# Layer 2's four x sums formed apart, a superblock ahead, and kept in DRAM

## The chip, the cores and the metric

The kernel runs on one core of one Trainium2 chip. The metric is device time in microseconds (us) of one execution. Before the change the median of three runs is 1597.66 us (1596.65 to 1598.69).

## The reference

A linear attention is followed by two MLPs. Softmaxes of q (over its head dimension) and k (over the sequence) give, per batch and head, `kv = k_s.T @ v` and `out = q_s @ kv`; the result is x, 4608 tokens by 512. Then

```python
h = x @ moe_w_in              # 512 x 2048
x = max(0.01 * h, h) @ moe_w_out
h = x @ moe2_w_in
out = (h / (1 + exp(-h))) @ moe2_w_out
```

All inputs and the output are float32. The kernel calls the four products layers 0, 1, 2 and 3.

## The kernel before

**Arithmetic.** An operand of a product is held as a high part (a rounded copy, ScalarE) and a low part (what is left, a VectorE subtraction), so a float32 product is three matmuls on TensorE: high by high, high by low, low by high. Layers 1, 2 and 3 are done as 2 x 2 blocks by a scheme with seven products in place of eight. Each of the seven products c takes one block, or one sum of blocks, of the weights and one of x. For layer 2's x, products 1, 2 and 3 take blocks as they are, and products 7, 5, 6 and 4 take sums: 7 = 3 - 5', 5 = 5' - 1, 6 = 3 - 5, 4 = 2 - 6, where 5' is the raw fourth block (`SUMS["x"]`, line 720; 11 and 12 are second copies of raw blocks 1 and 2).

**Tiling.** Tokens come in nine blocks of 512, and layers 1 and 2 take them in superblocks n = 0 to 4: four of two blocks, and a last one of one block. A full superblock has for layer 2 two operands per product (kq = 0, 1, written 6a and 6b below), the last has one. In layer 2 (`layer2`, lines 1007 to 1044) a superblock has four turns i; a turn has seven products, in the order 1, 2, 6, 5, 7, 4, 3, where product 1 of the next turn is put ahead of products 4 and 3 of this one. A product is 12 matmuls.

**x of layer 2.** Layer 1's result goes to DRAM (`store1`, line 994, into `x2d`). `x_all` (line 816) takes, for each superblock, an operand tile for each product and kq from the pool `r_x`, in the order 1, 5, 3, 2, 6, 7, 4; `operand` (line 776) spawns the loads (`fetch`, line 737), the sums (`sums`, line 746, into 128 x 512 work tiles of the pool `r_o`) and the split (`split2`, line 757): a ScalarE copy to the high half (`copy`, line 302), a VectorE subtraction to the low half (`sub`, line 298). Sums are VectorE operations of `add` (line 863). Raw blocks wait in the low halves of tiles (`HOME2`, line 730: the copies 11 and 12 go to tiles 5 and 4). There are six loads per kq.

`r_x` has 15 tiles once layer 1 runs out: eight called x, three g, and xs, xv and two xr. Layer 2 holds 14 of them (seven per kq) for all four turns of a superblock, and gives each pair back after its product in the last turn (line 1042). `r_o` has 16 tiles.

**What sets the order.** The program of every engine is written out in an order that a planner finds (`Queues`, lines 63 to 146). Each piece of work is a generator with a rank; it yields operations with an engine and a cost ("D" is the DMA queue at 0.73 us per 256 KB, plus 3.0 us to landing), waits for named events, and takes tiles. At each step the operation that can begin first is taken, and among equals the one of lowest rank (line 122). `yield rank(r)` sets the rank and holds nothing back (line 100). Engines then run in that order, and a semaphore holds an instruction until what it needs is there. All loads and stores are issued by SyncE (the SP queue), in order.

Other work of the same stretches: `convert3` (line 431) turns the last layer's weights into blocks, in layer 1's gaps, and its two `raw` tiles join `r_x` as xr when it ends (line 435); `weight` (line 798) loads and splits a weight when its room comes free; `blocks1`, `blocks2`, `plus` and `active` take products out of PSUM; `keep` (line 1095) stores layer 2's result to `gd`.

Of the kernel before, what the change touches and what calls it, by code (L numbers as in the profile page):

```python
# [9 lines left out]
F32 = mybir.dt.float32  # L10
# [4 lines left out]
ALU = mybir.AluOpType  # L15
# [31 lines left out]
def rank(r):  # L47
    return "rank", r


def op(*engines):
    return "op", engines


def wait(*keys):
    return "wait", keys


def get(ring):
    return "get", ring  # L60


class Queues:
# [14 lines left out]
    def spawn(self, rank, gen):  # L78
        self.tasks.append([rank, next(self.count), self.now, gen, None, 0.0, None])
        self.tasks.sort(key=lambda t: t[:2])  # L80
        self.step(next(t for t in self.tasks if t[3] is gen), None)
# [8 lines left out]
    def done(self, key):  # L90
        self.events[key] = self.now
# [111 lines left out]
def linear_attention_two_mlps(  # L203
# [24 lines left out]
    nc = tc.nc  # L228
    B, H, S, D = q.shape
    NT, DM = out.shape  # L230
    DFF = w_in1.shape[1]
    P = 128
    TB = 512
    NB = NT // TB
    NP = H // 2
    KD = DM // P
# [25 lines left out]
    NJ = len(supers)  # L262
    width = [len(s) * HB for s in supers]
    merge = [2 // len(s) for s in supers]
    gd1 = [tc.dram_tile([NG, 2, 4, P, len(s), HB], F32, name=f"gda{n}") for n, s in enumerate(supers)]
    gd = [tc.dram_tile([NG, 4, len(s), P, 2, HB], F32, name=f"gd{n}") for n, s in enumerate(supers)]
    x2d = [tc.dram_tile([KD, P, 2, w], F32, name=f"x2d{n}") for n, w in enumerate(width)]

    NKV = 8
    NV = 2 * (D + 1)  # L270
# [11 lines left out]
    done, spawn = qs.done, qs.spawn  # L282
# [410 lines left out]
    def act(j, f, h):  # L693
# [28 lines left out]
    }  # L722
    ORDER = (1, 2, 6, 7, 5, 3, 4)
# [3 lines left out]
    SECOND = (2, 5, 3)  # L727
    HOME = {3: (6, 1), 5: (7, 1), 2: (4, 1)}
    HOMES = HOME, {}
    HOME2 = {11: (5, 0), 12: (4, 1)}  # L730
    slot = {}

    def raw_of(key, c, home):
# [42 lines left out]
    def operand(keys, kind, r, order, srcs, give, home={}, used=(), each=0.0):  # L776

        def turn(c):
            return r + each * used.index(c) if c in used else r

        for key in keys:
            spawn(r, sums(key, kind, home, turn))
        for c in order:
            for key, src in zip(keys, srcs):
                yield rank(r)
                slot[key, c] = yield from give(c)
                done(("slot", key, c))
                for d in src:
                    if home.get(d, (d, 1))[0] == c:
                        spawn(r, fetch(key, d, home, src[d]))  # L790
                spawn(turn(c), split2(key, kind, c, home))
# [6 lines left out]
    def weight(l, i, c):  # L798
# [14 lines left out]
        src = wc[l][2 * i:2 * i + 2, :, PLANS[l][2].index(c)].rearrange("r p n -> p r n")  # L813
        yield from operand([key], "", weight_rank(l, i, c), (c,), [{c: src}], give)

    def x_all():
        for n in range(NJ):

            r, pm = at2[n, 0] - (5 if n else 4), merge[n]
            yield rank(r)  # L820
            yield wait(*(("x2", n, k, t) for k in range(0, KD, pm) for t in range(2)))
            keys, srcs = [], []
            for kq in range(2 // pm):
                keys.append(("x", 2, n, kq))
                srcs.append({})
                for c, k, t in ((1, 0, 0), (5, 0, 1), (2, 1, 0), (3, 1, 1)):
                    at = 2 * k + kq * pm
                    srcs[-1][c] = x2d[n][at:at + pm, :, t].rearrange("k p w -> p k w")
                    if c < 3:
                        srcs[-1][10 + c] = srcs[-1][c]  # L830
            yield from operand(keys, "x", r, (1, 5, 3, 2, 6, 7, 4), srcs, lend, home=HOME2, used=ORDER, each=0.5)

    def g1_all():
        for n in range(NJ):
            pm = merge[n]
            for g, (cs, kind) in enumerate(((FIRST, "b"), (SECOND, ""))):
                for i in range(NG):
                    for q_ in range(2 // pm):
                        at = at1[n, g, i, q_] - 4
                        yield rank(at)  # L840
                        fs = range(4 * i + 2 * q_, 4 * i + 2 * q_ + 2 * pm)
                        yield wait(*(("gd1", j, f) for j in supers[n] for f in fs))
                        src = {
                            c: gd1[n][i, q_ * pm:(q_ + 1) * pm, m].rearrange("z p j n -> p z (j n)")
                            for m, c in enumerate(KEPT1)
                        }
                        yield from operand(
                            [("x", 1, n, g, i, q_)], kind, at, cs, [src], lend, home=HOMES[g]
                        )
# [11 lines left out]
    def add(o, a, b, alu=ALU.add):  # L861
        yield op(("V", v_tt(TB)))
        nc.vector.tensor_tensor(out=o, in0=a, in1=b, op=alu)  # L863
# [81 lines left out]
                                    spawn(-100, blocks1(n, mb))  # L945

    def blocks1(n, m):
        key, pm = (1, n), merge[n]

        def product(c):  # L950
            yield wait(("p", 1, n, m, c))
            return banks[key, m, c]

        def room():
            return (yield get(r_o))

        def end(c):
            r_b.put(banks.pop((key, m, c)))

        p = yield from product(1)  # L960
        s = yield from room()
        yield op(("A", a_(TB)))
        copy("A", s, p)
        done(("kept", n, m))
        p = yield from product(6)
        yield from add(s, s, p)
        end(6)
        p = yield from product(7)
        u = yield from room()
        yield from add(u, s, p)  # L970
        end(7)
        p = yield from product(4)
        t = yield from room()
        yield from add(t, u, p)
        end(4)
        spawn(-100, store1(n, 2 + m * pm, 0, t))
        p = yield from product(2)
        t = yield from room()
        yield op(("A", a_(TB)))
        copy("A", t, p)  # L980
        banks.pop((key, m, 1))
        end(2)
        spawn(-100, store1(n, m * pm, 0, t))
        p = yield from product(5)
        yield from add(u, u, p)
        spawn(-100, store1(n, 2 + m * pm, 1, u))
        yield from add(s, s, p)
        end(5)
        p = yield from product(3)
        yield from add(s, s, p)  # L990
        end(3)
        spawn(-100, store1(n, m * pm, 1, s))

    def store1(n, k, t, o):
        pm = merge[n]
        yield op(("D", 0.73))
        nc.sync.dma_start(
            out=x2d[n][k:k + pm, :, t].rearrange("k p w -> p k w"), in_=o.rearrange("p (k w) -> p k w", k=pm)
        )
        yield wait()  # L1000
        r_o.put(o)
        done(("x2", n, k, t))

    INTO = {1: 1, 6: 1, 7: 1, 4: 1, 2: 2, 5: 5, 3: 5}
    AFTER = {6: 1, 7: 6, 4: 7, 3: 5}
# [170 lines left out]
    for j in range(NB):  # L1176
        for i in range(NG):
            at3[j, i] = t_
            t_ += 2

    def weight_rank(l, i, c):
        if l == 1:
            return at1[0, int(c in SECOND), i, 0] - 8
        return (at2[0, i] if l == 2 else at3[0, i]) - 8

    with tc.manual_schedule():
        nc.vector.memset(ones, 1.0)
        make_identity(nc, ident)
        nc.scalar.activation(out=small[0]["k"][:, 0:1], in_=ones, func=ACTF.Exp)
        for t_, t in sets:  # L1190
            t5 = t.rearrange("p (c h d) -> p c h d", c=5, h=2)
            nc.gpsimd.memset(t5[:, :, :, D:], 1.0)

            nc.gpsimd.memset(t_[SR:P, 512:640], 0.0)
            nc.gpsimd.memset(t5[SR:P, 4, :, 0:D], 0.0)
        nc.gpsimd.memset(kv_tile, 0.0)

        for n in range(NP):
            r = -40 + 5 * n
            spawn(r, k_task(n))  # L1200
            spawn(r + 1, q_task(n))
            spawn(r + 2, v_task(n))
        for n in range(NP, len(units)):
            b, j, p = units[n]
            r = -12 + 3 * p if j == 1 else step(j, 0) - 14 + 4 * p
            if b is not None:
                spawn(r, k_task(n))
                spawn(r, v_task(n))
            spawn(r, q_task(n))
        for f in range(NF):  # L1210
            spawn(-36 + 6 * f if f < 4 else step(0, f) - 4, split1(f))
            if f < NH:
                spawn(f, layer0(0, f))
        spawn(0, layer0_all())
        for t in (convert1, convert2, convert3):
            spawn(1000, t())
        spawn(0, later())
        for i, c in lead:
            spawn(weight_rank(1, i, c), weight(1, i, c))
        for l in (2, 3):  # L1220
            for i in range(NG):
                for c in ORDER:
                    spawn(weight_rank(l, i, c), weight(l, i, c))
        spawn(base[1] - 4, g1_all())
        spawn(base[2] - 5, x_all())
        spawn(base[3] - 4, g3_all())
        spawn(base[1], layers())
        qs.run()
# [30 lines left out]
```

## Time and profile before

| | |
|---|---|
| median of three runs | 1597.66 us |
| the profiled execution, its own time | 1598.44 us |
| its span in the trace | 1596.7 us |
| mean granted TensorE clock, share of full | 0.995 |
| layer 2's first matmul starts | 855.14 us |
| layer 3's first matmul starts | 1229.78 us |

Times in the rows are from the start of the span. In the timelines a row is "start, length, engine, line, operation, output <- input, tiles' shape, count", and a bracket is the time for which the engine had been idle and what ended it. PE is TensorE, DVE VectorE, ACT ScalarE, SPq the queue of SyncE that issues DMAs. A clock of 0.50 is the lower of TensorE's two levels, 1.2 GHz; 1.00 is 2.4 GHz.

### The profile page before, as it was taken

To read this page: it belongs to the slowest core of one execution; us is meant where nothing else is said; L and a number is where in the kernel's file an instruction comes from. 1 tells how busy PE (TensorE), PEld (TensorE's weight loads), DVE (VectorE), ACT (ScalarE), POOL (GpSimd) and SP (SyncE) were. 2 spreads that over 40 slices of the span, in tenths; PEclk is the share of its full clock that TensorE was granted. 3 is DMA by queue.
4 is the path that set the end of the run, shared out by engine and by line. 5 is a ranking of instruction groups with operands and counts; after the bars stand their busy time and mean duration, and the time that the engine had idled before them with its cause. 6 is when DMAs were issued, how large, how long until landed. Compare 5 with 4: busy or idle time off the path is not lost.

```text
span 1596.7 us, 26548 instructions
## 1 busy us (share of the span) xinstructions
PE 1548.6 (97%) x9088; PEld 1340.4 (84%) x9088; DVE 1093.9 (69%) x2046; ACT 893.5 (56%) x1965; POOL 39.4 (2%) x56
## 2 busy tenths in 40 slices
PE   5899999999999999999997999999999999999999
PEld 3687888888788888888887878787889999999998
DVE  8986756665656988888888352525267777777774
ACT  7778776685445544454556454545467444444442
POOL 2111000000000000000000000000000000000000
PEclk9999999999999999999999999999999999999999
DMA  8876778786789787878797353535369444444442
GB/s 236 267 200 179 227 228 255 227 269 194 240 268 312 234 293 217 273 219 268 230 323 269 106 185 106 185 106 175 108 195 303 133 131 133 132 133 127 134 128 70
DMA packets 281190, 320.01 MB, mean 200 GB/s; under 512 B 61408, under 2 KB 208352, under 8 KB 281056
## 3 DMA queue, kind: packets, MB, share of 16 engines
q1 hardware_dynamic: 281056, 318.32, 63.8%
q8 instruction: 72, 1.18, 0.3%
q14 instruction: 62, 0.51, 0.1%
HBM read 201.85 MB, written 116.39 MB: 199 GB/s over the span
## 4 chain that ended last, share of the span: by engine, by line
PE 90%; DVE 6%; DMA 2%; SPq 1%; issue 1%; ACT 0%; POOL 0%; DVEq 0%; POOLq 0%; ACTq 0%
PE b L1124 12%; PE h L1124 11%; PE h L1034 10%; PE b L931 10%; PE h L931 10%; PE b L1034 8%; PE h L665 8%; PE h L667 8%; PE h L666 8%; DVE o L863 2%; PE a L637 2%; DVE x L298 1%; PE a L520 1%; PE a L622 1%; DMA u<-in_k_dram 0%
## 5 line engine op out<-in xcount | busy, mean ns | idle before, releaser
L665 PE MATMUL h<-x,w 128*128 128x512 f32 x576 | 237.1, 412 | 1.9 <-ACT w L302 1.1
L666 PE MATMUL h<-x,w 128*128 128x512 f32 x576 | 224.8, 390 | 2.2 <-DVE x L298 1.6
L667 PE MATMUL h<-x,w 128*128 128x512 f32 x576 | 225.2, 391 | 0.4 <-DVE w L298 0.4
L302 ACT ACTIVATE x<-x 128x512 fp32r<-128x512 f32 x194 | 121.6, 630 | 156.8 <-DMA x<-gd 87.7
L863 DVE TENSOR_TENSOR o<-o,h 128x512 f32<-128x512 f32 x107 | 72.3, 686 | 129.1 <-ACT o L302 68.0
L698 ACT ACTIVATE o<-h 128x512 f32<-128x512 f32 x144 | 86.1, 598 | 116.4 <-PE h L667 107.4
L298 DVE TENSOR_TENSOR x<-x 128x512 fp32r<-128x512 f32 x194 | 129.6, 686 | 13.0 <-ACT x L302 10.2
L863 DVE TENSOR_TENSOR o<-o,b 128x512 f32<-128x512 f32 x118 | 79.6, 686 | 85.8 <-ACT o L302 35.4
L665 PEld LDWEIGHTS h<-x,w 128*128 128x128 f32 x576 | 108.4, 188 | 28.0 <-ACT x L645 1.8
L666 PEld LDWEIGHTS h<-x,w 128*128 128x128 f32 x576 | 108.5, 188 | 24.7 <-DVE x L298 3.2
L667 PEld LDWEIGHTS h<-x,w 128*128 128x128 f32 x576 | 108.1, 188 | 24.2 <-DVE w L298 0.8
L1034 PE MATMUL h<-x,a 128*128 128x512 f32 (+1 forms) x489 | 120.8, 379 | 6.9 <-DVE x L298 6.9
L931 PE MATMUL b<-x,a 128*128 128x512 f32 (+1 forms) x498 | 117.6, 374 | 1.2 <-DVE x L298 1.2
L931 PE MATMUL h<-x,a 128*128 128x512 f32 (+1 forms) x510 | 115.0, 364 | 0.5 <-DVE x L298 0.5
L1034 PEld LDWEIGHTS h<-x,a 128*128 128x128 f32 x489 | 88.7, 193 | 24.6 <-DVE x L298 7.7
L1124 PE MATMUL b<-a,x 128*128 128x256 f32 x816 | 107.2, 283 | 0.0
L931 PEld LDWEIGHTS b<-x,a 128*128 128x128 f32 x498 | 89.0, 188 | 18.0 <-DVE x L298 1.4
L1124 PEld LDWEIGHTS b<-a,x 128*128 128x128 f32 x816 | 102.0, 192 | 0.0
L1034 PE MATMUL b<-x,a 128*128 128x512 f32 (+1 forms) x423 | 98.4, 365 | 3.5 <-DVE x L298 3.5
L931 PEld LDWEIGHTS h<-x,a 128*128 128x128 f32 x510 | 88.1, 189 | 15.9 <-DVE x L298 0.7
L1124 PE MATMUL h<-a,x 128*128 128x256 f32 x768 | 100.8, 283 | 0.0
L302 ACT ACTIVATE x<-o 128x512 fp32r<-128x512 f32 x124 | 75.7, 625 | 42.0 <-DVE o L863 38.0
(165 smaller groups left out, 2975.9 us busy)
## 6 DMA issues: line engine op xcount, KB each, us to landing
x<-gda SPq DMA_DIRECT2D x152, 256.0 KB, 3.5
gda<-o SPq DMA_DIRECT2D x144, 256.0 KB, 2.8
gd<-o SPq DMA_DIRECT2D x144, 256.0 KB, 2.7
x<-gd SPq DMA_DIRECT2D x90, 256.0 KB, 2.7
a<-wc SPq DMA_DIRECT2D x84, 256.0 KB, 4.9
wc<-o SPq DMA_DIRECT2D x72, 256.0 KB, 3.1
raw<-in_moe_w_out_dram SPq DMA_DIRECT2D x32, 512.0 KB, 5.1
g<-gda SPq DMA_DIRECT2D x60, 256.0 KB, 3.4
```

The source lines that it names most:

```text
L298: engines[e].tensor_tensor(out=out_, in0=a, in1=b.bitcast(F32), op=ALU.subtract)
L302: nc.scalar.activation(out=out_, in_=in_, func=ACTF.Copy)
L520: nc.tensor.matmul(pk[o, 0:D + 1], lhsT=kc[:, o], rhs=vv[:, c, h * (D + 1):(h + 1) * (D + 1)], start=c == 0, stop=c == 4,)
L637: nc.tensor.matmul(po, lhsT=kv[bb, p], rhs=qT.rearrange("p (c t) -> p c t", c=4)[:, :, a:e], start=True, stop=True)
L665: nc.tensor.matmul(h, lhsT=w[:, 0, kk], rhs=x[:, 0], start=kk == 0, stop=False)
L666: nc.tensor.matmul(h, lhsT=w[:, 0, kk], rhs=x[:, 1], start=False, stop=False)
L667: nc.tensor.matmul(h, lhsT=w[:, 1, kk], rhs=x[:, 0], start=False, stop=kk == KD - 1)
L698: nc.scalar.activation(out=o, in_=h, func=ACTF.Prelu, alpha=0.01)
L863: nc.vector.tensor_tensor(out=o, in0=a, in1=b, op=alu)
L931: nc.tensor.matmul(banks[key, mb, c][:, mo * w_:(mo + 1) * w_], lhsT=w[:, a, at:at + P], rhs=x[:, b, z * w_:(z + 1) * w_], start=begin and ...
L1034: nc.tensor.matmul(bank[:, z * w_:(z + 1) * w_], lhsT=w4[:, a, rq * pm + z, kc], rhs=x[:, b, ko:ko + w_], start=INTO[c] == c and not (z or ...
L1124: nc.tensor.matmul(bank[:, m * HB:(m + 1) * HB], lhsT=s[:, a, at:at + P], rhs=x[:, b, r * HB:(r + 1) * HB], start=i + m + n == 0, stop=i = ...
```

## The change

`x2d` gets a place for each of the seven operands of a superblock and kq. Layer 1's blocks go to the places of 1, 5 (raw), 2 and 3. A new generator `presums` loads the raw blocks into `r_o` tiles, forms the four sums there, and stores each to its place, that of 5 over its raw block. `x_all` takes the operands in the order in which layer 2 uses them, each with one load of its own, one copy and one subtraction; `SUMS["x"]` and `HOME2` go.

```diff
-    x2d = [tc.dram_tile([KD, P, 2, w], F32, name=f"x2d{n}") for n, w in enumerate(width)]
+    x2d = [tc.dram_tile([2 // m, 7, P, TB], F32, name=f"x2d{n}") for n, m in enumerate(merge)]
...
-        "x": ((7, 3, 5, "-"), (5, 5, 11, "-"), (6, 3, 5, "-"), (4, 12, 6, "-")),
...
-    HOME2 = {11: (5, 0), 12: (4, 1)}
...
+    RAW2 = {(0, 0): 1, (0, 1): 5, (1, 0): 2, (1, 1): 3}
+
+    def presums():
+        for n in range(NJ):
+            for kq in range(2 // merge[n]):
+                yield rank(sum_rank(n, kq))
+                yield wait(*(("x2", n, kq, c) for c in RAW2.values()))
+                x = {}
+
+                def load(c):
+                    x[c] = yield get(r_o)
+                    yield op(("D", 0.73))
+                    nc.sync.dma_start(out=x[c], in_=x2d[n][kq, c - 1])
+
+                def keep2(c):
+                    yield op(("D", 0.73))
+                    nc.sync.dma_start(out=x2d[n][kq, c - 1], in_=x[c])
+                    yield wait()
+                    r_o.put(x.pop(c))
+                    done(("x3", n, kq, c))
+
+                yield from load(3)
+                yield from load(5)
+                yield from load(1)
+                yield wait()
+                x[7] = yield get(r_o)
+                yield from add(x[7], x[3], x[5], ALU.subtract)
+                yield from keep2(7)
+                yield from add(x[5], x[5], x[1], ALU.subtract)
+                r_o.put(x.pop(1))
+                yield from load(2)
+                yield wait()
+                yield from add(x[3], x[3], x[5], ALU.subtract)
+                yield from keep2(5)
+                x[6] = x.pop(3)
+                yield from add(x[2], x[2], x[6], ALU.subtract)
+                x[4] = x.pop(2)
+                yield from keep2(6)
+                yield from keep2(4)
+
     def x_all():
         for n in range(NJ):
-
-            r, pm = at2[n, 0] - (5 if n else 4), merge[n]
+            r = at2[n, 0] - (5 if n else 4)
             yield rank(r)
-            yield wait(*(("x2", n, k, t) for k in range(0, KD, pm) for t in range(2)))
-            keys, srcs = [], []
-            for kq in range(2 // pm):
-                keys.append(("x", 2, n, kq))
-                srcs.append({})
-                for c, k, t in ((1, 0, 0), (5, 0, 1), (2, 1, 0), (3, 1, 1)):
-                    at = 2 * k + kq * pm
-                    srcs[-1][c] = x2d[n][at:at + pm, :, t].rearrange("k p w -> p k w")
-                    if c < 3:
-                        srcs[-1][10 + c] = srcs[-1][c]
-            yield from operand(keys, "x", r, (1, 5, 3, 2, 6, 7, 4), srcs, lend, home=HOME2, used=ORDER, each=0.5)
+            kqs = range(2 // merge[n])
+            for c in (1, 2, 6, 5, 7, 4, 3):
+                for kq in kqs:
+                    yield wait(("x2" if c in (1, 2, 3) else "x3", n, kq, c))
+                    spawn(r, operand([("x", 2, n, kq)], "", r, (c,), [{c: x2d[n][kq, c - 1]}], lend))
...
-    def store1(n, k, t, o):
-        pm = merge[n]
+    def store1(n, m, k, t, o):
+        c = RAW2[k, t]
         yield op(("D", 0.73))
-        nc.sync.dma_start(
-            out=x2d[n][k:k + pm, :, t].rearrange("k p w -> p k w"), in_=o.rearrange("p (k w) -> p k w", k=pm)
-        )
+        nc.sync.dma_start(out=x2d[n][m, c - 1], in_=o)
         yield wait()
         r_o.put(o)
-        done(("x2", n, k, t))
+        done(("x2", n, m, c))
...
+    def sum_rank(n, kq):
+        return at1[2, 0, 0, 0] + 4 * kq if not n else at2[n - 1, kq]
+
...
+        spawn(sum_rank(0, 0), presums())
         spawn(base[2] - 5, x_all())
```

## Rows read from the trace of the kernel before

**Rows 1.** The page: busy times of the engines, and the chain's shares by engine.

```profile
PE 1548.6 (97%) x9088; PEld 1340.4 (84%) x9088; DVE 1093.9 (69%) x2046; ACT 893.5 (56%) x1965; POOL 39.4 (2%) x56
...
PE 90%; DVE 6%; DMA 2%; SPq 1%; issue 1%; ACT 0%; POOL 0%; DVEq 0%; POOLq 0%; ACTq 0%
```

**Rows 2.** Who PE waited for from 850 to 1235 us: total, times, longest.

```profile
PE h L1034 <- DVE x L298: 6.9, 2, 3.5
PE h L1034 <- DVE xr L298: 6.4, 1, 6.4
PE b L1034 <- DVE x L298: 3.5, 1, 3.5
PE b L1034 <- ACT o L302: 2.1, 1, 2.1
PE h L1034 <- ACT xr L302: 1.2, 1, 1.2
PE h L1034 <- DVE xv L298: 0.5, 1, 0.5
```

**Rows 3.** Timeline of PE: layer 2's ends, its first wait, and the next.

```profile
855.14 0.86 PE L1034 MATMUL h<-xs,a 128*128 128x512 f32 x3
...
869.70 1.22 PE L1034 MATMUL h<-xr,a 128*128 128x512 f32 x2 [6.44 <-DVE xr L298]
...
944.90 3.11 PE L1034 MATMUL b<-x,a 128*128 128x512 f32 x13
951.54 1.97 PE L1034 MATMUL b<-x,a 128*128 128x512 f32 x5 [3.53 <-DVE x L298]
...
1229.78 3.04 PE L1124 MATMUL b<-a,g 128*128 128x256 f32 x24
```

**Rows 4.** The chain in order of time: the pace of 512- and 256-column matmuls.

```profile
957.29 2.72 PE b L1034 x12
...
1205.69 2.88 PE b L1034 x24
```

**Rows 5.** Windows: length, then busy us (instructions) by engine, clock, DMA share, GB/s.

```profile
590.00:820.00 230.00, 229.51 (x1040) 191.03 (x1039) 191.26 (x316) 114.56 (x194) 0.00 (x0) 1.00 0.80 248
820.00:868.00 48.00, 40.37 (x307) 38.10 (x305) 43.18 (x72) 33.86 (x59) 0.00 (x0) 0.99 1.03 348
...
870.00:874.00 4.00, 4.00 (x11) 3.09 (x11) 3.51 (x7) 3.96 (x8) 0.00 (x0) 0.54 0.18 62
952.00:956.00 4.00, 4.00 (x13) 3.13 (x12) 3.09 (x6) 1.75 (x4) 0.00 (x0) 0.57 0.30 102
```

**Rows 6.** Timeline of DVE around the first two waits.

```profile
857.75 1.29 DVE L863 TENSOR_TENSOR o<-x,x 128x512 f32<-128x512 f32 x2
...
868.96 0.68 DVE L298 TENSOR_TENSOR xr<-o,xr 128x512 fp32r<-128x512 f32 x1
...
938.04 0.69 DVE L863 TENSOR_TENSOR o<-xr,xv 128x512 f32<-128x512 f32 x1 [1.14 <-DMA xr<-x2d]
938.65 0.68 DVE L863 TENSOR_TENSOR o<-o,h 128x512 f32<-128x512 f32 x1
...
950.20 0.68 DVE L863 TENSOR_TENSOR o<-x,o 128x512 f32<-128x512 f32 x1
950.80 1.28 DVE L298 TENSOR_TENSOR x<-o,x 128x512 fp32r<-128x512 f32 x2
```

**Rows 7.** Timeline of the SP queue between superblocks 0 and 1 of layer 2.

```profile
922.66 8.18 SPq L1098 DMA_DIRECT2D gd<-o  x8
930.93 1.39 SPq L742 DMA_DIRECT2D x<-x2d  x2
932.41 0.87 SPq L742 DMA_DIRECT2D xr<-x2d  x2
```

**Rows 8.** DMA issues: count, KB each, median us from issue to landing.

```profile
x2d<-o SPq DMA_DIRECT2D x36, 256.0 KB, 4.1
...
x<-x2d SPq DMA_DIRECT2D x28, 256.0 KB, 4.7
```

More of the change, by code (lines that the diff above doesn't have):

```diff
@@ L947, in blocks1 @@
     def blocks1(n, m):
-        key, pm = (1, n), merge[n]
+        key = 1, n
         def product(c):
@@ L975, in blocks1 @@
         end(4)
-        spawn(-100, store1(n, 2 + m * pm, 0, t))
+        spawn(-100, store1(n, m, 1, 0, t))
         p = yield from product(2)
@@ L982, in blocks1 @@
         end(2)
-        spawn(-100, store1(n, m * pm, 0, t))
+        spawn(-100, store1(n, m, 0, 0, t))
         p = yield from product(5)
         yield from add(u, u, p)
-        spawn(-100, store1(n, 2 + m * pm, 1, u))
+        spawn(-100, store1(n, m, 1, 1, u))
         yield from add(s, s, p)
@@ L991, in blocks1 @@
         end(3)
-        spawn(-100, store1(n, m * pm, 1, s))
-    def store1(n, k, t, o):
-        pm = merge[n]
+        spawn(-100, store1(n, m, 0, 1, s))
+    def store1(n, m, k, t, o):
+        c = RAW2[k, t]
         yield op(("D", 0.73))
-        nc.sync.dma_start(
-            out=x2d[n][k:k + pm, :, t].rearrange("k p w -> p k w"), in_=o.rearrange("p (k w) -> p k w", k=pm)
-        )
+        nc.sync.dma_start(out=x2d[n][m, c - 1], in_=o)
         yield wait()
         r_o.put(o)
-        done(("x2", n, k, t))
+        done(("x2", n, m, c))
     INTO = {1: 1, 6: 1, 7: 1, 4: 1, 2: 2, 5: 5, 3: 5}
```

## The prediction

> **What bounds the kernel.** The page comes first: PE is busy for 1548.6 of 1596.7 us and holds 90% of the chain [rows 1], so time is won only where PE stands still or runs at its lower clock. The list of who PE waited for, taken around layer 2, says where that is: 20.6 us, of which 18.5 us end with a copy or subtraction that makes an x operand and 2.1 us with a ScalarE read [rows 2].
>
> How much layer 2 loses in all follows from its ends, 855.14 and 1229.78: 374.64 us [rows 3]. Its work is four superblocks of 336 matmuls at 2.72/12 = 0.2267 us and one of 336 at 2.88/24 = 0.120 us [rows 4], 304.7 + 40.3 = 345.0 us. So 29.6 us are lost: 20.6 of idle time and 9.0 of slower matmuls. The windows show these 9.0: after the first wait the clock is 0.54 of full for 4 us and after the second 0.57 [rows 5]. Four long waits (6.44, 3.53 and the two behind the other 3.4 [rows 2, 3]) share them: 2.25 us each.
>
> The timelines show which operand is late. A superblock is four turns of seven products at 2.72 us. At 944.90 PE runs product 2 of superblock 1 (12 of that row's 13 matmuls), then begins product 6, and its first matmul that reads a low half stands still until 951.54 [rows 3]. Product 6's subtraction, begun at 950.80, ends a stretch in which DVE never stops: from 938.04, where the first sum starts as the raw block lands, to 950.80 [rows 6]. The eight sums of the superblock (four per kq) are in that stretch, the last of them right ahead at 950.20; besides them it holds eight subtractions and five of layer 2's own additions (counted in that timeline; its ends are shown). The next two changes of superblock repeat this, a superblock later each. The start of layer 2 is the same with weights in it: product 6 waits for a subtraction at 868.96, and eight sums stand ahead of it from 857.75 on [rows 6]. The change to the last superblock has no wait.
>
> **The change, part by part.**
>
> *The sums leave the change of superblock.* Eight VectorE instructions at 0.60 us (two in a row take 1.29, one 0.69 [rows 6]) are 4.8 us less ahead of product 6's subtraction. It is late by 3.53. So at the three inner changes the wait goes on this account alone, and with it the slow matmuls: 3 x (3.47 + 2.25) = 17.2 us, where 3.47 is (6.9 + 3.5)/3 [rows 2].
>
> *The operands are taken in the order of use.* What is late next would be a load. Tiles come back in the order 1, 2, 6, 5, 7, 4, 3, two per product, and there are 15 for 14, so each new operand takes the tile of its own predecessor or of the one before. Product 6b then gets its tile 16 us (six products) ahead of its use. A load lands in 4.7 us [rows 8], the copy and subtraction add 1.3, which leaves about 10 us. Before, tiles were given in the order 1, 5, 3, 2, 6, and two loads (blocks 5 and 3) and two sums stood in front of product 6.
>
> *SP queue.* Loads stand behind stores there: eight stores of `gd` block it from 922.66 to 930.84, and the loads follow at 930.93 and 932.41 [rows 7]. Such a block, 8.2 us, is inside the 10. I count 0; the other end is two such blocks in a row, 16.4 - 10 = 6.4 us at each change.
>
> *The start of layer 2* loses 0.5 + 1.2 + 6.4 of idle [rows 2] and 2.25 of clock, 10.3 us. Eight sums less are 4.8 us of the wait of 6.44, and the order of use puts product 6's subtraction ahead of those for 5, 7 and 4. But from 820 to 868 us DMA carries 348 GB/s and DVE is busy for 43.2 of 48 us [rows 5], and two more loads come in. I take 8 of the 10.3; the ends are 4.8 and 10.3.
>
> *What is added.* Nine pairs (n, kq) get four loads and four stores in work tiles, 72 DMAs, and 63 operand loads replace 54: 81 x 262,144 bytes = 21.2 MB. The 36 subtractions only move. Where to? Its rank does not hold `presums` back: a superblock's sums begin once layer 1 has stored its x and work tiles are free. From 590 to 820 us DVE is busy for 191 of 230 us and DMA carries 248 GB/s [rows 5]. Three superblocks add 24 x 0.60 = 14 us of DVE to 39 us of gaps, and 48 x 0.262 = 12.6 MB, 55 GB/s, which makes 303 of the 348 seen. PE takes its operands there from a pool of 15 tiles at one per 1.36 us (six matmuls), some 20 us ahead. This cover hides the loads, the SP issues and any wait of a store for its sum. Costed at 0 there. If the cover is gone, the work falls in 820 to 868 us, between the loads of layer 2's weights: 16 DMAs of one superblock at 0.262/0.348 = 0.75 us are 12 us. I take 3 us, nearer to the low end because the planner puts this work behind everything of lower rank; the ends are 0 and 12. `convert3` and the sums share work tiles and gaps, which is in the same range.
>
> *Chain of one pair.* Three load latencies and stores at 4.1 to 4.7 [rows 8], each store waited for before the next step: about 28 us, 57 for a superblock, against 76 us per superblock. Ready in time, if only just for superblock 1.
>
> *Left alone:* the ScalarE wait of 2.1 at layer 2's end.
>
> **Sum.** 17.2 + 8 - 3 = 22.2 us. The profiled execution took 1598.4, which gives 1576.2; it lies 0.8 above the median of 1597.66, so the median becomes 1575.5.
>
> **The rivals.**
>
> *The wait moves to the loads.* The 14 loads of a change all wait for their own tile, in order, behind stores that wait for ScalarE. For it: the block of 8.2 us [rows 7]. Against: 10 us of lead. Then half of the inner changes stays (8.6) and 5 of the start is won: 1597.7 - 8.6 - 5 + 3 = 1587.
>
> *Nothing is won.* If product 6 waits for its tile or for DVE's other work, the sums being hidden, the time stays at 1598. Against: the sum right ahead of the late subtraction [rows 6].
>
> *Slower: the sums land in the saturated stretch.* In layer 1 the sums have the last rank; if they find no gap until superblock 4, the sums of superblocks 1 to 3 (48 DMAs) run between 820 and 868 us, where DMA already carries 348 GB/s [rows 5]. Each costs 0.75 us there: 36 us, and weights for layer 2 come as much later: 1575.5 - 3 + 36 = 1609. It decides from some 34 of the 48 on, where 0.75 us each eat up the 25.2 won. Against: 39 us of DVE gaps and 100 GB/s of room before 820. The Trainium skill, page "DMA: Bandwidth & Descriptors", section Specifications, puts the limit of memory at about 358 GB/s per core; that speaks against adding bytes here, and the trace's 348 over 48 us agrees. By its figure the 48 DMAs are, as an estimate, 35 us, and the time would be 1608.
>
> *The change doesn't do what it says* in one respect: the sums need not be a superblock ahead, only early. This alters no number above.
>
> **How the numbers follow.** The forecast has 0.64 (its own range 1568 to 1584), the move to the loads 0.20, nothing won 0.06, slower 0.10. The low end of 1567 is all of the 29.6 us and 1 more; the range up to 1590 takes in most of the second case. About 0.2%, 3.2 us, is what a measurement can tell from no change. Faster 0.84, same 0.06, slower 0.10.
>
> **What would show it.** Right: no wait of PE for an x operand of over 1 us between 870 us and layer 2's end; clock 1.00 in all its windows; layer 2 in about 350 us; the four sums as VectorE instructions on work tiles, most of them before 820 us; DMA above 290 GB/s from 590 to 820 us; layer 1 ending within 3 us of 855. Wrong: a wait for the copy (not the subtraction) of an operand whose load was late; waits in layer 1 of over 5 us; or product 2 or 6 late once more although no sum is ahead of it.

## The result, and the profile after

The changed kernel takes 1576.59 us (median of four runs, 1574.92 to 1577.38) where the kernel before takes 1598.18 in runs beside it: a ratio of 0.986 (95% interval 0.984 to 0.988), 21.6 us less. The forecast was 1575.5 us, range 1567 to 1590. The profiled execution took 1576.41 us, its span is 1574.6.

First the page, parts 1 and 4, of the changed kernel, as [rows 1]:

```profile
PE 1543.8 (98%) x9088; PEld 1338.1 (85%) x9088; DVE 1092.3 (69%) x2046; ACT 893.9 (57%) x1965; POOL 39.5 (3%) x56
...
PE 94%; DMA 3%; DVE 2%; SPq 1%; ACT 0%; issue 0%; POOL 0%; DVEq 0%; ACTq 0%; POOLq 0%
```

PE's matmuls are as many as before and the span is 22 us shorter. VectorE has the same 2046 instructions: nothing was saved there, only moved.

Who PE waited for from 850 to 1235 us, as [rows 2]:

```profile
PE b L1063 <- ACT o L302: 1.7, 2, 1.4
```

Of six rows one is left, the ScalarE wait that the change does not touch. (Line numbers move by up to 33: layer 2's matmul L1034 is now L1063, layer 1's L931 is L962, layer 3's L1124 is L1153, `add` L863 is L894.)

The timeline of PE, as [rows 3]: layer 1's last superblock (the first 256-column product), the longest wait in it, and the first matmuls of layers 2 and 3.

```profile
814.76 1.60 PE L962 MATMUL h<-xs,a 128*128 128x256 f32 x12
...
843.32 1.58 PE L962 MATMUL h<-x,a 128*128 128x256 f32 x11 [1.43 <-DVE x L298]
...
860.58 0.86 PE L1063 MATMUL h<-xs,a 128*128 128x512 f32 x3
...
1207.83 3.04 PE L1153 MATMUL b<-a,x 128*128 128x256 f32 x24
```

Layer 2 takes 1207.83 - 860.58 = 347.25 us, where it took 374.64 [rows 3]: 27.4 us won. But it starts 5.4 us later. The last superblock of layer 1 takes 860.58 - 814.76 = 45.82 us; before, its first product stood at 812.52 and layer 2 followed at 855.14:

```profile
812.52 1.60 PE L931 MATMUL h<-xs,a 128*128 128x256 f32 x12
```

That is 42.62 us, so 3.2 us were lost there, and 2.2 us ahead of it. The 2.2 us are there in full when layer 1 begins, here and before:

```profile
510.12 2.88 PE L962 MATMUL b<-g,a 128*128 128x512 f32 x12
```
```profile
507.88 2.88 PE L931 MATMUL b<-g,a 128*128 128x512 f32 x12
```

The first load of a sum starts at 594.77, so the sums have no part in them (last section). 27.4 - 3.2 - 2.2 makes 22.0 of the 22.1 us by which the spans differ.

The windows, as [rows 5]: layer 1's steady part, the stretch of heavy DMA, and the first change of superblock in layer 2.

```profile
590.00:820.00 230.00, 230.00 (x1037) 191.33 (x1036) 197.56 (x326) 114.39 (x192) 0.00 (x0) 1.00 0.86 275
820.00:868.00 48.00, 44.04 (x327) 41.55 (x326) 42.41 (x73) 36.22 (x62) 0.00 (x0) 1.00 1.04 352
```
```profile
930.00:960.00 30.00, 30.00 (x134) 24.86 (x133) 17.02 (x27) 20.08 (x36) 0.00 (x0) 1.00 0.66 218
```

At the change PE is never idle and the clock is full. VectorE is busy for 17.0 of the 30 us, hardly less than before:

```profile
930.00:960.00 30.00, 26.47 (x110) 21.46 (x109) 17.70 (x29) 16.27 (x30) 0.00 (x0) 0.94 0.58 182
```

Sums of a later superblock run in this stretch now (`presums` stores some of them, L830, at 931.70 and 947.20 in the SP queue). What has gone is the unbroken row of work ahead of product 6's subtraction [rows 6].

The order there: the timelines of the SP queue and of DVE, as [rows 7] and [rows 6], and one row of PE.

```profile
917.19 8.23 SPq L1127 DMA_DIRECT2D gd<-o  x8
925.51 3.38 SPq L740 DMA_DIRECT2D x<-x2d  x6
```
```profile
923.97 0.69 DVE L298 TENSOR_TENSOR xv<-xv 128x512 fp32r<-128x512 f32 x1
...
931.45 1.29 DVE L298 TENSOR_TENSOR x<-x 128x512 fp32r<-128x512 f32 x2
...
935.45 0.69 DVE L298 TENSOR_TENSOR x<-x 128x512 fp32r<-128x512 f32 x1 [1.51 <-ACT x L302]
936.75 1.29 DVE L298 TENSOR_TENSOR x<-x 128x512 fp32r<-128x512 f32 x2 [0.61 <-ACT x L302]
```
```profile
939.48 0.84 PE L1063 MATMUL b<-xv,a 128*128 128x512 f32 x3
```

The block of eight stores still stands ahead of the loads and six loads follow at once. Product 2 begins on PE at 939.48 and takes 2a from the tile xv, whose subtraction stands at 923.97. By the order of the loads, the next subtractions are those of 2b and 6a, then 6b, then 5a and 5b: that of 6b ends at 935.45 + 0.69 = 936.1. Product 6, a product after product 2, asks for its first low half at 942.4. Its operands are 6 us early, where they were 3.5 late.

### The profile page after: what moved, and what is told of

The parts are those of the page before. It is cut to its first block, busy times and chain, and to the rows that moved or that the text cites. A ratio compares the mean times of both kernels' runs of the same rounds, so it can differ in the third digit from the quotient of the medians.

```text
span 1574.6 us, 26644 instructions
## 1 busy us (share of the span) xinstructions
PE 1543.8 (98%) x9088; PEld 1338.1 (85%) x9088; DVE 1092.3 (69%) x2046; ACT 893.9 (57%) x1965; POOL 39.5 (3%) x56
## 4 chain that ended last, share of the span: by engine, by line
PE 94%; DMA 3%; DVE 2%; SPq 1%; ACT 0%; issue 0%; POOL 0%; DVEq 0%; ACTq 0%; POOLq 0%
PE h L1063 12%; PE b L1153 12%; PE h L1153 11%; PE b L962 11%; PE h L962 10%; PE b L1063 9%; PE h L665 8%; PE h L667 8%; PE h L666 8%; PE a L637 2%; PE a L520 1%; DMA a<-wc 1%; PE a L622 1%; DMA rw<-in_moe_w_in_dram 1%; DMA x<-gda 0%; DMA u<-in_k_dram 0%
## 5 line engine op out<-in xcount | busy, mean ns | idle before, releaser
L302 ACT ACTIVATE x<-x 128x512 fp32r<-128x512 f32 x200 | 124.9, 630 | 135.2 <-DMA x<-gd 58.1
L894 DVE TENSOR_TENSOR o<-o,h 128x512 f32<-128x512 f32 x107 | 72.3, 686 | 113.3 <-ACT o L302 60.4
L894 DVE TENSOR_TENSOR o<-o,b 128x512 f32<-128x512 f32 x118 | 79.5, 686 | 79.4 <-ACT o L302 31.0
L962 PE MATMUL b<-x,a 128*128 128x512 f32 (+1 forms) x498 | 117.6, 374 | 0.4 <-DVE x L298 0.4
L1063 PE MATMUL h<-x,a 128*128 128x512 f32 (+1 forms) x492 | 117.6, 384 | 0.0
L962 PE MATMUL h<-x,a 128*128 128x512 f32 (+1 forms) x510 | 115.0, 364 | 1.9 <-DVE x L298 1.9
L1063 PEld LDWEIGHTS h<-x,a 128*128 128x128 f32 x492 | 90.8, 188 | 18.2
L1153 PE MATMUL h<-a,x 128*128 128x256 f32 x804 | 104.6, 283 | 0.0
L962 PEld LDWEIGHTS b<-x,a 128*128 128x128 f32 x498 | 89.0, 188 | 17.2 <-DVE x L298 0.6
L1153 PE MATMUL b<-a,x 128*128 128x256 f32 x804 | 103.6, 283 | 0.0
L962 PEld LDWEIGHTS h<-x,a 128*128 128x128 f32 x510 | 88.1, 189 | 17.6 <-DVE x L298 2.3
L1153 PEld LDWEIGHTS h<-a,x 128*128 128x128 f32 x804 | 100.1, 192 | 0.0
L1153 PEld LDWEIGHTS b<-a,x 128*128 128x128 f32 x804 | 99.6, 192 | 0.0
```

Of the source, the lines that this page charges most:

```text
L302: nc.scalar.activation(out=out_, in_=in_, func=ACTF.Copy)
L962: nc.tensor.matmul(banks[key, mb, c][:, mo * w_:(mo + 1) * w_], lhsT=w[:, a, at:at + P], rhs=x[:, b, z * w_:(z + 1) * w_], start=begin and ...
L1063: nc.tensor.matmul(bank[:, z * w_:(z + 1) * w_], lhsT=w4[:, a, rq * pm + z, kc], rhs=x[:, b, ko:ko + w_], start=INTO[c] == c and not (z or ...
L1153: nc.tensor.matmul(bank[:, m * HB:(m + 1) * HB], lhsT=s[:, a, at:at + P], rhs=x[:, b, r * HB:(r + 1) * HB], start=i + m + n == 0, stop=i = ...
```

## The experiments

Each row below is one kernel. "Last superblock" is the time from layer 1's first 256-column product to layer 2's first, "layer 2" that from its first matmul to layer 3's, both worked out from the profiled execution's timeline of PE; "convert3 ends" is the start of its last store in the SP queue.

| kernel | convert3 ends | last superblock | layer 2 | median of the runs |
|---|---|---|---|---|
| before | 821.84 | 42.62 | 374.64 | 1598.2 |
| changed | 834.64 | 45.82 | 347.25 | 1576.6 |
| after_again | 835.93 | 45.88 | 347.12 | 1575.4 |
| after_third | 833.49 | 45.94 | 346.88 | 1574.7 |
| old_order | 834.27 | 45.82 | 347.60 | 1576.2 |
| sums_back | 833.08 | 45.02 | 354.28 | 1581.7 |
| old_sums | 833.21 | 45.73 | 360.28 | 1589.3 |
| no_presums | 823.68 | 41.78 | 346.84 | 1571.9 |
| gate | 830.94 | 45.14 | 348.48 | 1575.8 |
| conv_first | 824.43 | 41.72 | 347.62 | 1571.6 |
| gate_conv | 821.12 | 41.55 | 347.05 | 1571.4 |
| conv_first_again | 824.95 | 42.03 | 347.06 | 1573.0 |
| conv_early | 696.30 | 40.31 | 347.18 | 1576.6 |

The kernel before took 1598.1 us beside after_again, old_order, sums_back and no_presums, 1595.9 beside old_sums, gate, conv_first and gate_conv, and 1598.3 beside after_third, conv_first_again and conv_early. Medians of two of these groups can thus differ by 2 us for that alone; within a group they are compared directly.

**What removed the waits: the sums' time, or the order of the tiles?** The change does both, so each was undone alone, and then both. The measure:

> The changed kernel once more, as the measure for the other runs of this group. 1575 to 1578 us; layer 2 from its first matmul to layer 3's in 347 us, no wait of PE in it over 1.5 us; layer 1's last superblock with 3.5 to 4.5 us of waits.

Measured: 1575.43 us. Layer 2 is as expected, with one wait of 1.0 us; the last superblock has 3.3 us of waits, a little less than expected.

*The old order, sums apart.*

```diff
-            for c in (1, 2, 6, 5, 7, 4, 3):
+            for c in (1, 5, 3, 2, 6, 7, 4):
```

> The sums stay apart and in DRAM, but the operand tiles are given in the old order 1, 5, 3, 2, 6, 7, 4. Theory A (the eight sums in VectorE's queue ahead of product 6's subtraction were the wait): the three inner changes of superblock stay without waits, the start of layer 2 may lose up to 5 us, 1577 to 1582 us. Theory B (the order in which tiles are given decides, the sums would have fitted): waits of 3 to 6 us and the lower clock behind them are back at each change, 1588 to 1598 us.

Measured: 1576.22 us, 0.9867 of the kernel before (0.985 to 0.988). Who PE waited for from 850 to 1235 us:

```profile
PE b L1063 <- DVE x L298: 0.8, 1, 0.8
PE b L1063 <- ACT o L302: 0.7, 1, 0.7
```

The 0.8 us lie at the start of layer 2; the changes of superblock have none. So theory A holds as far as it says that taking the sums away is enough. The order by itself is worth 0.8 us of waiting here.

*The order of use, with the sums' time put back.*

```diff
+        **{f"r{c}": ((c, 20 + c, 20 + c, "m"),) for c in (6, 5, 7, 4)},
...
+                    d = c if c in (1, 2, 3) else 20 + c
+                    kind, home = ("", {}) if d == c else (f"r{c}", {d: (c, 1)})
-                    spawn(r, operand([("x", 2, n, kq)], "", r, (c,), [{c: x2d[n][kq, c - 1]}], lend))
+                    spawn(r, operand([("x", 2, n, kq)], kind, r, (c,), [{d: x2d[n][kq, c - 1]}], lend, home=home))
```

> The order of use stays, and each operand of products 6, 5, 7 and 4 gets one VectorE instruction of a sum's size (the maximum of the loaded operand with itself) between its load and its copy, in a work tile as the sums had it: eight per change, 4.8 us of VectorE. Theory A: waits return at the changes, 2 to 4 us each with 2 us of lower clock, 1586 to 1594 us. Theory B: six products (16 us) of lead hold a load of 4.7, a sum of 0.7 and a split of 1.3 us, no wait over 1 us at the inner changes, 1576 to 1581 us.

Measured: 1581.72 us (0.9899, 0.9885 to 0.9914), close above theory B's figures and below theory A's. The waits, from 850 to 1235 us, and the timeline of DVE around the first:

```profile
PE h L1066 <- DVE xs L298: 4.8, 1, 4.8
PE b L1066 <- ACT o L302: 1.1, 1, 1.1
```
```profile
859.86 2.49 DVE L897 TENSOR_TENSOR o<-x 128x512 f32<-128x512 f32 x4
862.26 1.29 DVE L897 TENSOR_TENSOR o<-g 128x512 f32<-128x512 f32 x2
863.47 0.69 DVE L298 TENSOR_TENSOR xs<-xs 128x512 fp32r<-128x512 f32 x1
```

No wait at the changes of superblock: there theory A, read strictly, is wrong, for the same VectorE time does no harm in the order of use. At the start of layer 2 it does: six of the put-back instructions stand ahead of product 1's subtraction at 863.47, PE waits 4.8 us, and layer 2 is 7 us longer.

*Both undone.* The two edits together.

> Both at once: tiles given in the old order, and one VectorE instruction of a sum's size between load and copy of each operand of products 6, 5, 7 and 4. If VectorE's time in the old order made the wait, waits of 2 to 4 us return at the three inner changes of superblock, 1590 to 1596 us. If it was the chain (product 6 needing two sums of three loaded blocks, all behind one block of stores), which is not in this run, the inner changes stay without waits and only the start of layer 2 loses, as in the run with the sums' time put back: 1578 to 1584 us.

Measured: 1589.32 us (0.9957, 0.9943 to 0.9972), just below the first answer. The waits from 850 to 1235 us:

```profile
PE h L1066 <- DVE xs L298: 5.0, 1, 5.0
PE h L1066 <- DVE g L298: 2.4, 1, 2.4
PE h L1066 <- DVE xr L298: 1.4, 1, 1.4
PE b L1066 <- DVE x L298: 0.9, 1, 0.9
PE b L1066 <- ACT o L302: 0.7, 1, 0.7
```

The second, third and fourth are the three changes of superblock (at 1028.92, 1108.13 and 949.38 us), and they are back: 4.7 us together, where the kernel before had 10.4 [rows 2]. So neither half makes the wait alone; VectorE's eight instructions and the old order make it together, in less than half its size. What made the rest is not shown. A likely cause is the chain, which no run here puts back: product 6's operand needed three loaded blocks and two sums, one behind the other, and here every put-back instruction needs one block. In [rows 6] the first sum begins only as a raw block lands, at 938.04.

**What the change costs: 3 us in layer 1's last superblock.**

*No sums at all.*

```diff
-        spawn(sum_rank(0, 0), presums())
...
-                    yield wait(("x2" if c in (1, 2, 3) else "x3", n, kq, c))
-                    spawn(r, operand([("x", 2, n, kq)], "", r, (c,), [{c: x2d[n][kq, c - 1]}], lend))
+                    raw = {6: 3, 7: 5, 4: 2}.get(c, c)
+                    yield wait(("x2", n, kq, raw))
+                    spawn(r, operand([("x", 2, n, kq)], "", r, (c,), [{c: x2d[n][kq, raw - 1]}], lend))
```

> No sums are formed at all: products 6, 7, 5 and 4 of layer 2 get raw blocks 3, 5', 5' and 2, so layer 2 computes something else, in the same time. 72 DMAs and 36 subtractions fall away. Theory C (the sums cost what layer 1's last superblock lost, by putting convert3's last pair into it): its waits go from 4 back to 1.7 us, 1573 to 1574 us. Theory D (what it lost comes from the two more operand loads and the new order at the start of layer 2): unchanged, 1576 to 1577 us.

Measured: 1571.90 us (0.9838, 0.9823 to 0.9853). The last superblock takes 41.78 us, convert3 ends 11 us earlier, layer 2 is as long as before the edit. So forming the sums costs 3.5 us against the changed kernel beside it (1575.43), and that superblock, 4.1 us shorter than there (45.88), accounts for all of it. Theory D is out: the loads and the order at layer 2's start are the same here.

*Which of the sums, and through what?* In layer 1 the sums of superblock 0 and one pair of superblock 1 ran. Two edits:

```diff
+                if n:
+                    yield wait(("p", 1, NJ - 1, 0, 3))
                 yield rank(sum_rank(n, kq))
```

> The sums of superblocks 1 to 4 wait for the end of layer 1; those of superblock 0 stay. Theory C (sums in layer 1 push convert3's last pair into the last superblock): convert3's last store comes between 824 and 832 us in place of 835, layer 1's last superblock takes 43 to 45 us in place of 45.8, 1573 to 1575 us; superblock 1's sums then start at 860 us and end near 917, still ahead of their loads at 925. Theory E (only the amount of DMA in layer 1 counts): 8 DMAs less of 24, a third of the 4 us back, 1574 us. Failure: waits at superblock 1's change of several us.

Measured: 1575.80 us (0.9876, 0.986 to 0.989), above both theories' times. convert3 ends 4 us earlier, as theory C had it, but the last superblock is only 0.7 us shorter.

```diff
-        return at1[2, 0, 0, 0] + 4 * kq if not n else at2[n - 1, kq]
+        return base[1] + 60 + kq if not n else at2[n - 1, kq]
```

> Superblock 0's sums rank behind convert3 in place of ahead of it; no gate. Theory C: convert3's last store comes near 824 us again, layer 1's last superblock takes 42 to 43 us, 1572 to 1574 us, unless superblock 0's sums come too late for the start of layer 2 (waits there, 1576 to 1582 us). Theory E: the DMAs are the same, 1575 to 1577 us.

Measured: 1571.57 us (0.9845, 0.983 to 0.986), 4.2 us less than gate beside it, and the last superblock is as short as with no sums. The timelines of PE, and the last stores of convert3 in the SP queue, here and in the changed kernel:

```profile
813.57 1.60 PE L962 MATMUL b<-xs,a 128*128 128x256 f32 x12
...
855.29 0.86 PE L1063 MATMUL h<-xs,a 128*128 128x512 f32 x3
```
```profile
824.43 0.32 SPq L415 DMA_DIRECT2D wc<-o  x1
```
```profile
834.64 0.32 SPq L415 DMA_DIRECT2D wc<-o  x1
```

and the window of layer 1's steady part:

```profile
590.00:820.00 230.00, 229.87 (x1039) 191.19 (x1038) 199.37 (x329) 114.91 (x195) 0.00 (x0) 1.00 0.86 275
```

The same 275 GB/s as in the changed kernel, and yet the loss is gone. It is not the bytes, then (theory E), but who goes first: with superblock 0's sums ahead of it, convert3's last pair was still at work at 834 us, in the stretch where DMA carries 352 GB/s and VectorE is busy for 42.4 of 48 us. How its work there makes PE wait is not separated further. In the changed kernel's chain, the longest wait (PE at 843.32) goes back over VectorE and ScalarE to two loads:

```profile
821.19 6.43 DMA a<-wc
...
827.69 6.88 DMA x<-gda
```

Loads of these two kinds take 5.1 and 3.9 us by the median of the page.

> Both: superblock 0's sums behind convert3, those of 1 to 4 after layer 1. Theory C: 1571.5 to 1573 us, as much as forming no sums at all (1571.9). Theory E: 1574 us.

Measured: 1571.44 us (0.9848, 0.9833 to 0.9863): the gate adds nothing. Against the gate alone, which differs by the one line and ran beside it, it is 4.4 us faster, and the runs do not overlap (1570.71 to 1573.72 against 1575.46 to 1577.67).

**Is that a better kernel?** Both on one chip:

> The changed kernel, beside the next run on one chip: 1575 to 1577 us, as before.

> Superblock 0's sums behind convert3, again, beside the changed kernel: 3 to 5 us below it, 1570.5 to 1572.5 us. If the 4 us of the run before were a difference between chips, under 1.5 us below it.

Measured: 1574.65 us (1574.12 to 1575.83) and 1572.97 us (1570.84 to 1575.56). The medians are 1.7 us apart, less than expected, and the runs overlap. In the profiled executions the last superblock is 3.9 us shorter (45.94 against 42.03), but layer 1 began 0.9 us later (509.83 against 508.90), long before anything that the line touches. So the line is worth 4 us in that superblock; in the time it was 4.4 us in the gated pair, and this pair by itself doesn't tell it from nothing.

> As the last, and convert3's ranks 28 lower, so that it goes ahead of nearly all of layer 1's operands: if what is left in layer 1's last superblock (0.4 us of waits) is still convert3, 0.3 to 0.6 us faster, 1571 us; if convert3's earlier work now stands ahead of layer 1's operands, waits in layer 1's superblocks 1 to 3, which have none, and 1572 to 1580 us.

```diff
-        yield from convert(3, lambda r: base[1] + 28 + 4 * r)
+        yield from convert(3, lambda r: base[1] + 4 * r)
```

Measured: 1576.55 us, 3.6 us above conv_first_again beside it, whose line it has too. convert3 now ends at 696 us and the last superblock is the shortest of all, 40.3 us, but layer 1 pays for it earlier, as the second answer had it:

```profile
669.83 1.22 PE L962 MATMUL b<-x,a 128*128 128x512 f32 x2 [3.50 <-DVE x L298]
695.87 1.45 PE L962 MATMUL h<-xs,a 128*128 128x512 f32 x5 [1.26 <-DVE xs L298]
```

## Why the prediction was right

**The sum** came within 1.1 us of the median, in part by luck: the start of layer 2 gave 2.3 us more than was counted, and 2.2 us were lost ahead of layer 1, before anything that the change adds.

**The three inner changes** were to give 17.2 us, on account of the sums alone. They have no wait and full clock, and the run with the old order shows that taking the sums away was enough. The reason given, 4.8 us of VectorE time ahead of the subtraction, is right only in part: with that time put back, in the old order, the three waits are 4.7 us and not 10.4. More than half of what was won hung on something that the step does not name and that no run isolates. The step also left out that the order alone would have held the sums' VectorE time.

**The start of layer 2** was taken at 8 of 10.3 us. It has no wait, so all 10.3 came; with the three changes that makes 27.5, and 27.4 were measured. The step was too careful by 2.3 us.

**The lead of the loads** was put at 10 us for product 6b and was 6. The block of stores took 8.2 us as in [rows 7], but cost 6b little: its tile came free as the last product 6 of the superblock before ended, at 925.9, and its load was the third of the six issued from 925.51 on. These landed in 3.6 to 4.9 us, so 6b was there by 932. Its copy came later, behind other work of ScalarE that the step had at nothing:

```profile
934.80 0.62 ACT L302 ACTIVATE x<-x 128x512 fp32r<-128x512 f32 x1
```

The rival in which the wait moves to the loads was nearer than the text had it, but did not come.

**What is added** was put at 3 us between 820 and 868 us and came to 3.2. The place was right, the size by luck, and the cause wrong: against the kernel without sums it is 4.0 us (45.82 against 41.78), of which the other parts of the change gave 0.8 back (42.62 before). The step said that the planner puts the sums "behind everything of lower rank", and the rival that they have "the last rank" in layer 1. For superblock 0 that misreads the ranks: its sums stand two superblocks of layer 1 past the layer's beginning, some 30 in rank, while convert3's last four pairs stand at 44 to 56. So the sums went ahead of convert3, and convert3 into the full stretch. The price per DMA had no part in it: between 820 and 868 us DMA carries 352 GB/s against 348 before [rows 5], and of the sums' DMAs a single store is issued there. The sign "layer 1 ending within 3 us of 855" failed with this: layer 2 begins at 860.58, 5.4 us later, 3.2 of them from here.

**Where the sums run** was wrong. Most were expected before 820 us, with DMA above 290 GB/s; it was 275, and of 36 stores of sums 11 were out by then. The first pair took from 594.8 to 651 us and not 28. Three of the nine pairs began in layer 1, the rest filled the gaps of layer 2: those of superblock 2 are stored by 981.4 us, some 20 us ahead of most of their loads. That they were ready 20 us ahead, and not a superblock, did no harm.

**Slower** had its chance for the sums of superblocks 1 to 3 in the full stretch. They were not there: one of their stores falls between 820 and 868 us, at 863, and their next loads start at 868.4, behind that stretch.

## What to carry to other kernels

Work that stands between a resource coming free and its next use is worth moving even if its total stays the same: here VectorE kept all its instructions, and 27 us went when the eight sums that each critical operand stood behind were formed elsewhere. Their time on the engine was less than half of that wait at the changes; that a sum also has to wait for the loads it reads may be the rest, which was not tested. When such work becomes background, look at what else is background: the new work took the gaps of an older task that had a deadline, and one line that puts the two in the right order is worth another 4 us there. A lead that looks like 10 us on paper was 6 in the trace, since the copy behind the load also has to wait for its engine.

## What was not expected of the chip

The first 100 us differ between executions of the same program, in part by TensorE's clock. The windows of the profiled execution of the changed kernel, and of the third run of it:

```profile
0.00:100.00 100.00, 78.58 (x442) 57.08 (x443) 86.57 (x202) 73.36 (x198) 17.71 (x37) 0.98 0.84 242
...
41.00:44.00 3.00, 3.00 (x9) 2.32 (x8) 2.90 (x10) 1.67 (x4) 1.52 (x2) 0.50 0.06 14
```
```profile
0.00:100.00 100.00, 77.70 (x449) 56.49 (x449) 87.69 (x205) 74.62 (x205) 17.70 (x37) 1.00 0.86 245
```

In the first the clock is at its lower level, 0.50, from 41 to 44 us, and matmuls start 0.43 us apart and not 0.23, behind waits of 0.69 and 1.28 us that the other execution has at the same two matmuls. Layer 1 begins at 510.12 us in the first and at 508.90 in the other.

Not all of it is the clock. The matmul behind the first of these waits, in the changed kernel and in the kernel before:

```profile
38.84 0.50 PE L665 MATMUL h<-x,w 128*128 128x512 f32 x1 [0.69 <-ACT x L645]
```
```profile
37.41 0.49 PE L665 MATMUL h<-x,w 128*128 128x512 f32 x1 [0.69 <-ACT x L645]
```

Of the 2.2 us by which the changed kernel is behind when layer 1 begins, 1.4 are there before the clock falls; where they come from was not followed up. In the third run this matmul starts at 38.38, 1.0 us behind the kernel before, with the clock at 1.00 in all of the 100 us. Medians of four runs of kernels that differ by 2 us should be read with that in mind.
